# Four rows per partition in the q and k loads, a second matmul 24 steps behind the first, and loads four quads ahead

## The chip, the cores and the metric

The kernel runs on one core of a Trainium2 chip. The metric is the device time of one execution in microseconds (us). The kernel before takes 485.05 us (median of three runs, 484.16 to 485.57). The engines are called as the profile calls them: PE is TensorE's matmuls, PEld its weight loads, DVE is VectorE, ACT is ScalarE, POOL is GpSimd, and SP is the engine that issues the stores.

## The reference

Windowed attention with 32 global tokens per batch feeds a two-layer block with a quick GELU. The global tokens attend to everything; the 512 local tokens of each head attend to the global ones and to a window of 32 on both sides.

```python
# B=8, H=8 heads, Sl=512 local tokens, Sg=32 global tokens, D=64; d_model=512, d_ff=2048
k_all = concat([k_g, k_l]);  v_all = concat([v_g, v_l])
out_g = softmax(scale * q_g @ k_all.T) @ v_all
s_ll  = where(abs(i - j) <= 32, scale * q_l @ k_l.T, -1e9)
out_l = softmax(concat([scale * q_l @ k_g.T, s_ll])) @ concat([v_g, v_l])
x = concat([out_g, out_l])            # 8 * 544 = 4352 tokens of 512
h = x @ w_in
out = (h * sigmoid(1.702 * h)) @ w_out
```

## The kernel before

The kernel works on "quads", four heads of one batch, 16 quads in all. The batches' attention is interleaved with the two big matmuls of the block before it: a "block" is 512 tokens, a "step" is 128 of the 2048 hidden features. There are 8.5 blocks of 16 steps.

The loads put 16 consecutive rows of k (or q) of one head into one partition, 2 KB per partition, one DMA issue for each tensor:

```python
    qf = q_l.rearrange("b (u j) (r t) d -> (b u) (j r) (t d)", j=4, t=16)
    kf = k_l.rearrange("b (u j) (r t) d -> (b u) (j r) (t d)", j=4, t=16)
    ...
    def load(Q):
        rk = ld.tile([128, 16 * D], BF16, name="rk")
        nc.gpsimd.dma_start(out=rk, in_=kf[Q])
        rq = ld.tile([128, 16 * D], BF16, name="rq")
        nc.gpsimd.dma_start(out=rq, in_=qf[Q])
```

The scores need k and q with the features on the partitions. DVE's stream transpose turns every block of 32x32 elements. A block holds the rows `r` of one `t`, so its results belong 16 elements apart in the sequence. They are written with a stride of 16 bf16 elements, 32 bytes:

```python
    def quad(Q):
        ...
        kT = att.tile([128, 2, Sl], BF16, name="kT")
        qT = att.tile([128, 2, Sl], BF16, name="qT")
        for dst, src in ((kT, rk), (qT, rq)):
            nc.vector.transpose(
                dst.rearrange("p h (r t) -> p h t r", t=16),
                src.rearrange("p (t h d) -> p h t d", t=16, h=2),
            )
        ... # s = k.q on PE, exp on ACT, mask on DVE, sums and values on PE, xT = ov * rs on DVE
```

The two big matmuls need DVE as well. Each step fills a PSUM buffer `hp` (there are two), ACT takes its tanh, and DVE makes `gT` from both. Only when `gT` is written is `hp` free for the next step but one:

```python
    def h_step(i, fc):
        ...
        hp = psH.tile([128, TB], F32, name="hp")           # two buffers
        for kc in range(NKC):                               # four matmuls of 128x512
            nc.tensor.matmul(hp[:, :n], lhsT=w_in_sb[:, kc, ...], rhs=xT[:, kc, t0 : t0 + n], ...)
        nc.scalar.activation(th[:, :n], hp[:, :n], AF.Tanh, scale=0.851)
        nc.vector.scalar_tensor_tensor(gTs[i][:, fc, :n], in0=th[:, :n], scalar=1.0, in1=hp[:, :n], ...)

    for i in range(NBK + 1):
        ...
        for st in range(FC):                                # 16 steps
            if i < NBK: h_step(i, st)
            if i > 0:   o_step(i - 1, st)                   # second matmul, 16 steps behind
            ...                                             # and a piece of the next batch's attention
```

The softmax here doesn't subtract the row's maximum and nothing guards it: scores larger than these inputs give would overflow.

## Time and profile before

| | before |
|---|---|
| time | 485.05 us |
| span of the profiled execution | 482.6 us |
| mean granted clock of PE | 0.88 |
| PE busy | 363.7 us (75%) |
| DVE busy | 340.5 us (71%) |
| POOL busy | 112.5 us (23%) |

No engine is full over the whole span, so the average names no limit. One has to look at the stages. The first lines are of the page of the kernel before: busy time of the engines (share of the span, x instructions), then the span in 40 slices (busy tenths, and the clock granted to PE in tenths), then the chain of waits that ended last.

```profile
PE 363.7 (75%) x2913; PEld 184.5 (38%) x2960; DVE 340.5 (71%) x412; ACT 165.6 (34%) x307; POOL 112.5 (23%) x154
PE   0585476764677977599577977599559999999995
PEclk9995595786897997799887998799797999999999
PE 55%; DVE 33%; issue 7%; ACT 3%; DMA 1%; DVEq 0%; ACTq 0%; POOLq 0%
```

PE is full only in the last fifth, where no attention is left. Until then its clock drops again and again. The windows view of the same kernel shows this as three stages: block 0 with what precedes it, blocks 1 to 5, and the rest. Its columns are the window, its length, the busy time of PE, PEld, DVE, ACT and POOL with their instructions, the granted clock, the share of the DMA engines and GB/s.

```profile
0.00:124.00 124.00, 68.37 (x594) 36.27 (x602) 103.44 (x110) 31.38 (x57) 81.23 (x108) 0.78 0.88 96
124.00:383.10 259.10, 202.21 (x1685) 100.87 (x1714) 195.51 (x230) 92.99 (x171) 31.31 (x46) 0.88 0.28 42
383.10:482.60 99.50, 93.13 (x635) 47.40 (x644) 41.53 (x75) 41.28 (x79) 0.00 (x0) 1.00 0.11 41
```

The lines of the groups view give busy time and mean ns of one, then the engine's idle time just before them and what ended it.

```profile
L304 PE MATMUL hp<-xT,w_in_sb 128*128 128x512 bf16 (+1 forms) x535 | 154.2, 401 | 77.9 <-DVE gT L308 65.9
L196 DVE STREAM_TRANSPOSE kT<-rk 128x1024 bf16<-128x1024 bf16 x16 | 72.3, 4519 | 2.8 <-DMA rk<-in_k_l_dram 1.4
L196 DVE STREAM_TRANSPOSE qT<-rq 128x1024 bf16<-128x1024 bf16 x16 | 73.3, 4580 | 0.0
L74 POOL DMA_DIRECT2D rk<-in_k_l_dram x16 | 9.3, 581 | 70.4 <-DVE kT L196 66.6
L76 POOL DMA_DIRECT2D rq<-in_q_l_dram x16 | 8.9, 554 | 34.1 <-DVE qT L196 29.3
```

The 32 transposes take 4.5 us each, 146 us of DVE. PE waits 65.9 us for `gT`. How the one makes the other is seen in the timeline (start, us, engine and line, operation, and in brackets the idle time before it). First a pair of transposes on DVE, then what such a pair does to PE elsewhere:

```profile
282.20 0.68 DVE L308 SCALAR_TENSOR_TENSOR gT<-th,hp 128x512 bf16<-128x512 f32 x1
282.80 4.53 DVE L196 STREAM_TRANSPOSE kT<-rk 128x1024 bf16<-128x1024 bf16 x1
286.98 4.63 DVE L196 STREAM_TRANSPOSE qT<-rq 128x1024 bf16<-128x1024 bf16 x1
291.26 1.06 DVE L242 TENSOR_TENSOR e_2728<-e_2728,mask 128x1408 bf16<-128x1408 bf16 x1
292.25 0.66 DVE L308 SCALAR_TENSOR_TENSOR gT<-th,hp 128x512 bf16<-128x512 f32 x1
```

```profile
231.41 1.03 PE L320 MATMUL op<-w_out_sb,gT 128*128 128x512 bf16 x4
238.40 1.86 PE L304 MATMUL hp<-xT,w_in_sb 128*128 128x512 bf16 x4 [5.97 <-DVE gT L308]
```

For 9.4 us (from 282.88 to 292.25) DVE writes no `gT`, PE stands for 5.97 us, and the four matmuls after it take 1.86 us instead of 1.03. There are two such pairs in a block. So a block with transposes takes 52 to 55 us. The start of a block is read from its first tanh in the timeline, less 0.9 us.

### The profile page before, as it was taken

How to read it: one execution, taken by the hardware profiler on the slowest of the kernel's cores; microseconds unless marked ns; L12 is line 12 of the kernel's file. 1: busy time of each engine (PE TensorE's matmuls, PEld its weight loads, DVE VectorE, ACT ScalarE, POOL GpSimd, SP SyncE). 2: the span in 40 equal slices, each digit the busy share in tenths (PEclk: the TensorE clock that was granted, in tenths of full speed). 3: DMA queues.
4: the chain of work that ended last, by engine and by line, in shares of the span. 5: the costliest groups of instructions: out<-in, count | busy, mean ns of one | idle time of the engine just before them, and what ended most of it. 6: DMA issues, size and time to landing. Idle time of an engine off the chain costs nothing.

```text
span 482.6 us, 7101 instructions
## 1 busy us (share of the span) xinstructions
PE 363.7 (75%) x2913; PEld 184.5 (38%) x2960; DVE 340.5 (71%) x412; ACT 165.6 (34%) x307; POOL 112.5 (23%) x154
## 2 busy tenths in 40 slices
PE   0585476764677977599577977599559999999995
PEld 0253133332233533255233543255224555444552
DVE  7957869998986677866986778876796566633330
ACT  1330153231341372225331372126231374334341
POOL 9655992196101300022001210022000000000000
PEclk9995595786897997799887998799797999999999
DMA  9999894090513432344302433044000100011111
GB/s 116 113 141 198 111 118 57 2 109 6 61 34 58 47 46 57 66 45 45 67 7 58 50 43 64 22 46 46 22 24 0 45 23 23 24 42 46 44 45 65
DMA packets 55905, 26.96 MB, mean 56 GB/s; under 512 B 44352, under 2 KB 46400, under 8 KB 55872
## 3 DMA queue, kind: packets, MB, share of 16 engines
q0 software_dynamic: 50976, 17.58, 34.5%
q1 hardware_dynamic: 4896, 8.92, 4.9%
q8 instruction: 23, 0.38, 0.3%
q14 instruction: 10, 0.08, 0.1%
HBM read 35.13 MB, written 8.91 MB: 91 GB/s over the span
## 4 chain that ended last, share of the span: by engine, by line
PE 55%; DVE 33%; issue 7%; ACT 3%; DMA 1%; DVEq 0%; ACTq 0%; POOLq 0%
PE op L320 21%; PE hp L304 21%; DVE qT L196 15%; DVE kT L196 9%; PE ov L263 4%; DVE gT L308 3%; PE s L214 3%; PE ov L256 2%; PE s L236 2%; DVE e_1041 L242 2%; PE og L280 2%; DVE xT L276 1%; DMA rk<-in_k_l_dram 1%; DVE xg L288 1%; ACT ob L324 1%
## 5 line engine op out<-in xcount | busy, mean ns | idle before, releaser
L304 PE MATMUL hp<-xT,w_in_sb 128*128 128x512 bf16 (+1 forms) x535 | 154.2, 401 | 77.9 <-DVE gT L308 65.9
L307 ACT ACTIVATE th<-hp 128x512 f32<-128x512 f32 (+1 forms) x144 | 83.2, 579 | 240.3 <-PE hp L304 240.2
L320 PE MATMUL op<-w_out_sb,gT 128*128 128x512 bf16 x538 | 148.0, 398 | 2.0 <-ACT ob L324 1.4
L308 DVE SCALAR_TENSOR_TENSOR gT<-th,hp 128x512 bf16<-128x512 f32 (+1 forms) x144 | 94.0, 655 | 76.5 <-ACT th L307 75.9
L304 PEld LDWEIGHTS <-w_in_sb 128*128 128x128 bf16 x576 | 54.8, 102 | 137.8 <-issue 95.0
L320 PEld LDWEIGHTS <-gT 128*128 128x128 bf16 x544 | 55.5, 102 | 69.4 <-issue 14.7
L196 DVE STREAM_TRANSPOSE kT<-rk 128x1024 bf16<-128x1024 bf16 x16 | 72.3, 4519 | 2.8 <-DMA rk<-in_k_l_dram 1.4
L196 DVE STREAM_TRANSPOSE qT<-rq 128x1024 bf16<-128x1024 bf16 x16 | 73.3, 4580 | 0.0
L214 PE MATMUL s<-qT,kT 32*128 32x160 bf16 (+1 forms) x512 | 28.2, 263 | 29.3 <-DVE qT L196 29.3
L214 PEld LDWEIGHTS <-kT 32*128 32x128 bf16 x512 | 15.0, 100 | 48.1 <-issue 23.3
L276 DVE TENSOR_TENSOR xT<-ov,rs 128x512 bf16<-128x512 f32 x32 | 22.1, 690 | 11.8 <-PE ov L263 11.7
L324 ACT ACTIVATE ob<-op 128x512 f32<-128x512 f32 x34 | 20.6, 605 | 15.2 <-PE op L320 15.2
L74 POOL DMA_DIRECT2D rk<-in_k_l_dram x16 | 9.3, 581 | 70.4 <-DVE kT L196 66.6
L84 POOL DMA_DIRECT2D v_89<-in_v_l_dram x16 | 11.9, 754 | 49.2 <-PE og L282 48.4
L288 DVE TENSOR_SCALAR xg<-og,rg 32x64 bf16<-32x64 f32 x64 | 17.9, 280 | 1.2
L270 DVE STREAM_TRANSPOSE sT<-ov 128x512 f32<-128x512 f32 x16 | 11.6, 725 | 7.6 <-PE ov L263 7.6
L76 POOL DMA_DIRECT2D rq<-in_q_l_dram x16 | 8.9, 554 | 34.1 <-DVE qT L196 29.3
L84 POOL DMA_DIRECT2D v_91<-in_v_l_dram x16 | 12.0, 768 | 20.6 <-PE og L282 20.6
L256 PEld LDWEIGHTS <-vgU 128*128 128x128 bf16 x128 | 12.4, 111 | 11.0 <-issue 5.9
L84 POOL DMA_DIRECT2D v_87<-in_v_l_dram x16 | 12.1, 796 | 16.9 <-PE og L282 16.9
L236 PE MATMUL s<-qgBD,kT 128*128 128x128 bf16 x128 | 15.7, 242 | 0.0
L84 POOL DMA_DIRECT2D v_85<-in_v_l_dram x16 | 12.0, 778 | 15.7 <-PE og L282 15.7
(335 smaller groups left out, 346.7 us busy)
## 6 DMA issues: line engine op xcount, KB each, us to landing
out_dram<-ob SPq DMA_DIRECT2D x34, 256.0 KB, 2.0
rk<-in_k_l_dram POOLq DMA_DIRECT2D x16, 256.0 KB, 4.5
rq<-in_q_l_dram POOLq DMA_DIRECT2D x16, 256.0 KB, 3.8
w_in_sb<-in_moe_w_in_dram POOLq DMA_DIRECT2D x8, 256.0 KB, 13.2
w_out_sb<-in_moe_w_out_dram POOLq DMA_DIRECT2D x4, 512.0 KB, 10.8
v_85<-in_v_l_dram POOLq DMA_DIRECT2D x16, 64.0 KB, 3.1
v_87<-in_v_l_dram POOLq DMA_DIRECT2D x16, 64.0 KB, 3.3
v_89<-in_v_l_dram POOLq DMA_DIRECT2D x16, 64.0 KB, 2.8
```

The source lines that it names most:

```text
L84: nc.gpsimd.dma_start(out=v[:, :, j * D : (j + 1) * D], in_=vf[Q, j])
L196: nc.vector.transpose(dst.rearrange("p h (r t) -> p h t r", t=16), src.rearrange("p (t h d) -> p h t d", t=16, h=2),)
L214: nc.tensor.matmul(ps[j][:, col : col + wd], lhsT=kT[p, h, 128 * c : 128 * c + 128], rhs=qT[p, h, q0 : q0 + wd], start=(h == 0), stop=(h = ...
L236: nc.tensor.matmul(o, lhsT=l(h), rhs=r(h), start=(h == 0), stop=(h == 1), skip_group_check=True)
L256: nc.tensor.matmul(ov[:, q0 : q0 + wd], lhsT=lg, rhs=e, start=(i == 0), stop=False, skip_group_check=True)
L276: nc.vector.tensor_mul(xT[:, 2 * u + h, t0 + Sg : t0 + S], ov, rs)
L288: nc.vector.tensor_scalar_mul(xg[p, :], og[p, j * D : (j + 1) * D], rg[p, j : j + 1])
L304: nc.tensor.matmul(hp[:, :n], lhsT=w_in_sb[:, kc, fc * 128 : (fc + 1) * 128], rhs=xT[:, kc, t0 : t0 + n], start=(kc == 0), stop=(kc == NKC ...
L307: nc.scalar.activation(th[:, :n], hp[:, :n], AF.Tanh, scale=0.851)
L308: nc.vector.scalar_tensor_tensor(gTs[i][:, fc, :n], in0=th[:, :n], scalar=1.0, in1=hp[:, :n], op0=ALU.add, op1=ALU.mult)
L320: nc.tensor.matmul(ops[i], lhsT=gTs[i][:, fc, tci * 128 : tci * 128 + 128], rhs=w_out_sb[:, fc, :], start=(fc == 0), stop=(fc == FC - 1))
L324: nc.scalar.activation(ob, ops[i], AF.Copy, scale=0.5)
```

## The change

Its intent is to make the transposes cheap. Four rows instead of 16 lie in a partition, so the results of one 32x32 block belong four elements apart: the write stride falls from 32 to 8 bytes. Since a tensor's rows of a quad are now in four pieces per partition, each load becomes four issues of 64 KB. Around it, loads are issued four quads ahead instead of two, the second matmul runs 24 steps behind the first instead of 16, `xg` is scaled on ACT instead of DVE, `gT` has three buffers instead of two, and the global tokens' tables are kept for three batches instead of all eight, with their last load after `w_out`.

```diff
-    kf = k_l.rearrange("b (u j) (r t) d -> (b u) (j r) (t d)", j=4, t=16)
+    kf = k_l.rearrange("b (u j) (n r t) d -> (b u) j r n (t d)", j=4, n=4, t=4)
...  # q_l likewise; pool "ld" 3 -> 4 buffers
     def load(Q):
-        rk = ld.tile([128, 16 * D], BF16, name="rk")
-        nc.gpsimd.dma_start(out=rk, in_=kf[Q])
...
+        for name, src in (("rk", kf), ("rq", qf)):
+            r = ld.tile([128, 4, 4 * D], BF16, name=name)
+            for n in range(4):
+                nc.gpsimd.dma_start(out=r[:, n, :], in_=src[Q, :, :, n, :])
...
         for dst, src in ((kT, rk), (qT, rq)):
             nc.vector.transpose(
-                dst.rearrange("p h (r t) -> p h t r", t=16),
-                src.rearrange("p (t h d) -> p h t d", t=16, h=2),
+                dst.rearrange("p h (n r t) -> p h n t r", n=4, t=4),
+                src.rearrange("p n (t h d) -> p h n t d", t=4, h=2),
             )
...
-    load_g(2, NQ)
     load(2)
+    load_g(2, 4)
     load_v(2)
+    load(3)
+    load_v(3)
     for g4 in range(4):
         nc.gpsimd.dma_start(out=w_out_sb[...], ...)
-    transpose_g(2, NQ)
+    load_g(4, NQ)
+    transpose_g(2, 4)
...
-        if Q + 2 < NQ and Q + 2 not in loaded:
-            load(Q + 2)
-            load_v(Q + 2)
+        if Q + 4 < NQ:
+            load(Q + 4)                       # and load_v(Q + 4) at the quad's end
...
-            nc.vector.tensor_scalar_mul(xg[p, :], og[p, ...], rg[p, j : j + 1])
+            nc.scalar.activation(xg[p, :], og[p, ...], AF.Copy, scale=rg[p, j : j + 1])
...
+    LAG = 24
+    for k in range(NBK * FC + LAG):
+        i, st = divmod(k, FC)
...
+            h_step(i, st)
+        if 0 <= k - LAG < NBK * FC:
+            o_step(*divmod(k - LAG, FC))
```

More of the change, by code (lines that the diff above doesn't have):

```diff
@@ L54 @@
     wts = ctx.enter_context(tc.tile_pool(name="wts", bufs=1))
-    ld = ctx.enter_context(tc.tile_pool(name="ld", bufs=3))
+    ld = ctx.enter_context(tc.tile_pool(name="ld", bufs=4))
     att = ctx.enter_context(tc.tile_pool(name="att", bufs=2))
@@ L61 @@
     psO = ctx.enter_context(tc.tile_pool(name="psO", bufs=1, space=bass.MemoryType.PSUM))
-    qf = q_l.rearrange("b (u j) (r t) d -> (b u) (j r) (t d)", j=4, t=16)
-    kf = k_l.rearrange("b (u j) (r t) d -> (b u) (j r) (t d)", j=4, t=16)
+    qf = q_l.rearrange("b (u j) (n r t) d -> (b u) j r n (t d)", j=4, n=4, t=4)
+    kf = k_l.rearrange("b (u j) (n r t) d -> (b u) j r n (t d)", j=4, n=4, t=4)
     vf = v_l.rearrange("b (u j) (c p) d -> (b u) j p c d", j=4, p=128)
@@ L72, in load @@
     def load(Q):
-        rk = ld.tile([128, 16 * D], BF16, name="rk")
-        nc.gpsimd.dma_start(out=rk, in_=kf[Q])
-        rq = ld.tile([128, 16 * D], BF16, name="rq")
-        nc.gpsimd.dma_start(out=rq, in_=qf[Q])
-        loaded[Q] = [rk, rq, None]
+        got = []
+        for name, src in (("rk", kf), ("rq", qf)):
+            r = ld.tile([128, 4, 4 * D], BF16, name=name)
+            for n in range(4):
+                nc.gpsimd.dma_start(out=r[:, n, :], in_=src[Q, :, :, n, :])
+            got.append(r)
+        loaded[Q] = got + [None]
     vtiles = []
@@ L132 @@
     kgT = consts.tile([128, NQ, 2, 32], BF16)
-    qgBD = consts.tile([128, NQ, 2, 128], BF16)
-    kgBD = consts.tile([128, NQ, 2, 128], BF16)
-    vgU = consts.tile([128, NQ, 2, 128], BF16)
-    vgBD = consts.tile([128, NQ, 4 * D + 4], BF16)
-    for j in range(4):
-        nc.vector.tensor_copy(vgBD[:, :, 4 * D + j : 4 * D + j + 1],
-                              bdm[:, j : j + 1, 0:1].to_broadcast([128, NQ, 1]))
+    GB = []
+    for i in range(3):
+        kgBD = consts.tile([128, 2, 2, 128], BF16, name="kgBD%d" % i)
+        qgBD = consts.tile([128, 2, 2, 128], BF16, name="qgBD%d" % i)
+        vgU = consts.tile([128, 2, 2, 128], BF16, name="vgU%d" % i)
+        vgBD = consts.tile([128, 2, 4 * D + 4], BF16, name="vgBD%d" % i)
+        for j in range(4):
+            nc.vector.tensor_copy(vgBD[:, :, 4 * D + j : 4 * D + j + 1],
+                                  bdm[:, j : j + 1, 0:1].to_broadcast([128, 2, 1]))
+        GB.append((kgBD, qgBD, vgU, vgBD))
     def transpose_g(lo, hi):
@@ L156, in bd @@
             )
-        m = lambda t: t[:, qs].rearrange("p a h c -> p (a h) c")
-        bd(m(kgBD), m(kgT), 4, 32)
-        bd(m(qgBD), m(qgT), 4, 32)
+        kgBD, qgBD, vgU, vgBD = GB[b % 3]
+        m = lambda t: t.rearrange("p a h c -> p (a h) c")
+        bd(m(kgBD), m(kgT[:, qs]), 4, 32)
+        bd(m(qgBD), m(qgT[:, qs]), 4, 32)
         bd(m(vgU), rvg[:, qs, :].rearrange("p a (h d) -> p (a h) d", h=2), 4, 32)
-        bd(vgBD[:, qs, : 4 * D], rvg[:, qs, :], 2, D)
+        bd(vgBD[:, :, : 4 * D], rvg[:, qs, :], 2, D)
     transpose_g(0, 2)
@@ L181 @@
         )
-    transpose_g(2, NQ)
-    expand_g(1, nc.gpsimd)
+    load_g(4, NQ)
+    transpose_g(2, 4)
+    expand_g(1, nc.vector)
     xT = consts.tile([128, NKC, n_tokens], BF16)
@@ L191, in quad @@
         rk, rq, v = loaded[Q]
+        kgBD, qgBD, vgU, vgBD = GB[b % 3]
         t0 = b * S
@@ L196, in quad @@
             nc.vector.transpose(
-                dst.rearrange("p h (r t) -> p h t r", t=16),
-                src.rearrange("p (t h d) -> p h t d", t=16, h=2),
-            )
-        if u == 0 and b + 2 < B:
-            expand_g(b + 2, nc.gpsimd)
-        if Q + 2 < NQ and Q + 2 not in loaded:
-            load(Q + 2)
-            load_v(Q + 2)
+                dst.rearrange("p h (n r t) -> p h n t r", n=4, t=4),
+                src.rearrange("p n (t h d) -> p h n t d", t=4, h=2),
+            )
+        if Q + 4 < NQ:
+            load(Q + 4)
         E = []
@@ L224, in quad @@
                 full.append((ps[i][:, LW : LW + 128], lambda h, c=c: kT[:, h, 128 * c : 128 * c + 128],
-                             lambda h: qgBD[:, Q, h, :]))
-            kgl = lambda h: kgBD[:, Q, h, :]
+                             lambda h: qgBD[:, u, h, :]))
+            kgl = lambda h: kgBD[:, u, h, :]
             if rnd == 0:
-                full.append((ps[2][:, LW : LW + 128], kgl, lambda h: qgBD[:, Q, h, :]))
+                full.append((ps[2][:, LW : LW + 128], kgl, lambda h: qgBD[:, u, h, :]))
                 full.append((ps[2][:, 480:512], kgl, lambda h: qT[:, h, 480:512]))
@@ L253, in quad @@
             h = unit - 1
-            lg = onesBD if unit == 0 else vgU[:, Q, h, :]
+            lg = onesBD if unit == 0 else vgU[:, u, h, :]
             for i, (e, q0, wd) in enumerate(pieces):
@@ L281, in quad @@
                              start=(c == 0), stop=False)
-        nc.tensor.matmul(og, lhsT=E[0][:, 2, LW : LW + 128], rhs=vgBD[:, Q, :], start=False, stop=True)
+        nc.tensor.matmul(og, lhsT=E[0][:, 2, LW : LW + 128], rhs=vgBD[:, u, :], start=False, stop=True)
         rg = att.tile([128, 4], F32, name="rg")
@@ L287, in quad @@
             p = slice(32 * j, 32 * j + 32)
-            nc.vector.tensor_scalar_mul(xg[p, :], og[p, j * D : (j + 1) * D], rg[p, j : j + 1])
+            nc.scalar.activation(xg[p, :], og[p, j * D : (j + 1) * D], AF.Copy, scale=rg[p, j : j + 1])
         nc.vector.transpose(xT[:, 2 * u : 2 * u + 2, t0 : t0 + Sg],
                             xg.rearrange("p (h d) -> p h d", h=2))
+        if Q + 4 < NQ:
+            load_v(Q + 4)
         yield
@@ L300, in h_step @@
         if fc == 0:
-            gTs[i] = moe.tile([128, FC, TB], BF16, name="gT")
+            gTs[i] = moe.tile([128, FC, TB], BF16, name="gT", bufs=3)
         hp = psH.tile([128, TB], F32, name="hp")
@@ L328, in batch @@
     def batch(b):
+        if b == 1:
+            transpose_g(4, NQ)
+        if 1 <= b < B - 1:
+            expand_g(b + 1, nc.gpsimd)
         a, c = quad(2 * b), quad(2 * b + 1)
@@ L331, in batch @@
             yield next(g, None)
+    LAG = 24
+    NP = 12
     for _ in batch(0):
         pass
-    for i in range(NBK + 1):
-        g = batch(i + 1) if i + 1 < B else iter(())
-        done = 0
-        for st in range(FC):
-            if i < NBK:
-                h_step(i, st)
-            if i > 0:
-                o_step(i - 1, st)
-            while done * FC < (st + 1) * 12 and done < 12:
-                next(g, None)
-                done += 1
+    g = iter(())
+    for k in range(NBK * FC + LAG):
+        i, st = divmod(k, FC)
+        if st == 0:
+            g = batch(i + 1) if i + 1 < B else iter(())
+            done = 0
+        if i < NBK:
+            h_step(i, st)
+        if 0 <= k - LAG < NBK * FC:
+            o_step(*divmod(k - LAG, FC))
+        while done * FC < (st + 1) * NP and done < NP:
+            next(g, None)
+            done += 1
 _INS = ['q_l', 'k_l', 'v_l', 'q_g', 'k_g', 'v_g', 'moe_w_in', 'moe_w_out']
```

## The prediction

> **What bounds the kernel now.** Neither engine is full (page: PE busy 75%, DVE 71%), but two stages differ. From about 115 us to 384 us every 512-token block takes 52 to 55 us. A block without transposes (384 to 420 us in the timeline) takes only 36.5 us, with TensorE busy throughout: 32 groups of four 128x512 matmuls at 0.863 us (27.6 us) plus about 9.3 us of attention matmuls. So TensorE's floor is about 37 us per block. The other 17 us are DVE's: the groups view has 32 stream transposes at 4.52 and 4.58 us; they run in pairs, 8.8 us in which no gT is written, so hp's two PSUM buffers stay full. The waits view has PE hp waiting for DVE gT 65.9 us in 14 waits, up to 6.4 us. After each stall the clock is low: four matmuls take 1.86 us instead of 1.03. That is 2 x (6 + about 2.6) = 17 us per block. The page "TensorE: Matmul & The Clock Gate", Part 1, says that an idle window of about 3.4 us lowers the clock; the trace agrees.
>
> **What the change does.**
> - Transposes. They now write with a 32-byte stride, 4.4 ns per element; the dense 128x896 kgT transpose took 1.10 us, 1.2 ns per element. The Trainium skill ("SBUF — State Buffer", note on cachelines) says that lines have 16 bytes and need two hits each for full rate: an 8-byte stride gives two. No run here shows it yet. Estimate: 1.25 us each, 105 us less DVE work in all. A pair then takes 2.5 us, and gT is again written before TensorE needs its buffer.
> - xg moves to ScalarE: 64 x 0.28 us off DVE, about 64 x 0.22 us onto ScalarE (34% busy): free.
> - Loads: q and k become 128 issues instead of 32, about 0.55 us each: 53 us more on GpSimd (23% busy), harmless in steady state. At the start w_in is issued some 7 us later. DMA engine time hardly grows (a 2 KB packet took 217 ns, four of 512 B about 4 x 60).
> - Lag 24 instead of 16: TensorE's work is the same; eight steps of the second matmul move from the start to the end, where psO's single buffer costs about 0.7 us per four steps. It lets w_out land later.
>
> **Sum.** Batch 0: first block's matmuls in earnest at about 44 us instead of 57, as four of its transposes fall from 4.5 to 1.25 us and the next pair no longer delays it. Blocks 0 and 1, 57 to 170 us now, I put at 44 to 108: limited by loads (w_out and the fourth batch's q and k landing near 70 us) and DVE. Blocks 2 to 6: 5 x 37.5. Block 7 27.6, block 8 21, the last 16 steps 17, store 2: 363. Frictions (GpSimd's multiplies blocking DVE's mask multiplies, as in the 8.2 us one; small PSUM waits): about 9. Predicted 372 us, 8 in 10 between 353 and 399. Faster by over 2% 0.97, within 2% 0.02, slower 0.01.
>
> **What would show it.** Groups view: transposes 1.1 to 1.5 us. Waits: PE hp for DVE gT under 15 us. Timeline: 37 to 39 us per block, granted clock mean near 0.95. The chain of waits: over 80% PE, DVE under 12%. TensorE still mostly busy at about 310 to 340 us.
>
> **What would make it wrong.** Transposes at about 2.3 us (two lines still cost): some 20 us more. DVE queued behind the late global-token transposes (their load is now last): 10 to 20 us more. Four issues per tensor starving the first two blocks of data. Or start stages that overlap better than I think: 355.

## The result, and the profile after

The changed kernel takes 413.26 us (median of four runs, 412.90 to 413.52), and its result is right. The ratio to the kernel before is 0.8515 (95% interval 0.8495 to 0.8536). Ratios are computed as the mean time of one kernel's fast runs over that of the other's of the same rounds, so they are not quite the ratio of the medians quoted. The direction was right, and the time lies outside the predicted range of 353 to 399 us.

The lines of the page of the changed kernel that answer to those of before, with the row of POOL added:

```profile
PE 343.2 (83%) x2911; PEld 177.2 (43%) x2960; DVE 252.0 (61%) x362; ACT 184.0 (45%) x371; POOL 179.6 (44%) x249
PE   0665597677979987998899889988999999999985
POOL 8973993799999999445734002200000000000000
PEclk9999759699889998999999999999999999999999
PE 47%; POOL 19%; DVE 12%; DMA 8%; issue 7%; ACT 6%; DVEq 0%; ACTq 0%; POOLq 0%
```

The clock is nearly recovered (mean 0.963 after 0.88). DVE's part of the chain has fallen from 33% to 12%. POOL, which was not in it at all, has 19% and is nearly full for the first 40% of the span: it is busy for 114.88 of the 134.70 us before block 2. The windows view of the changed kernel, cut at the starts of blocks 2 and 7 (the DMA share adds up the times of all packets, so it can pass 1):

```profile
0.00:134.70 134.70, 91.77 (x844) 48.37 (x857) 93.35 (x143) 51.78 (x106) 114.88 (x166) 0.90 1.06 98
134.70:340.70 206.00, 188.28 (x1756) 97.83 (x1785) 140.19 (x187) 108.92 (x221) 64.77 (x84) 0.99 0.39 51
340.70:411.50 70.80, 63.13 (x313) 31.04 (x318) 18.46 (x34) 23.28 (x46) 0.00 (x0) 1.00 0.13 49
```

The prediction had put the start of block 2 at 108 us and these five blocks at 187.5 us. The groups of the changed kernel:

```profile
L313 PE MATMUL hp<-xT,w_in_sb 128*128 128x512 bf16 (+1 forms) x533 | 144.5, 380 | 31.1 <-DVE gT L317 27.3
L206 DVE STREAM_TRANSPOSE kT<-rk 128x1024 bf16<-128x1024 bf16 x16 | 39.5, 2471 | 10.4 <-DMA rk<-in_k_l_dram 8.7
L206 DVE STREAM_TRANSPOSE qT<-rq 128x1024 bf16<-128x1024 bf16 x16 | 39.4, 2465 | 0.8 <-DMA rq<-in_q_l_dram 0.7
L77 POOL DMA_DIRECT2D rk<-in_k_l_dram x64 | 43.6, 690 | 17.6 <-DVE kT L206 6.6
L77 POOL DMA_DIRECT2D rq<-in_q_l_dram x64 | 42.4, 669 | 9.0 <-DMA w_in_sb<-in_moe_w_in_dram 4.3
```

A transpose takes 2.47 us, twice the 1.25 us of the prediction. The loads of q and k take 86 us of POOL, after 18.2 us before (9.3 + 8.9). The timeline of a pair of transposes, DVE first and then PE:

```profile
225.78 2.47 DVE L206 STREAM_TRANSPOSE kT<-rk 128x1024 bf16<-128x1024 bf16 x1
228.04 2.49 DVE L206 STREAM_TRANSPOSE qT<-rq 128x1024 bf16<-128x1024 bf16 x1
230.34 0.91 DVE L249 TENSOR_TENSOR e_2807<-e_2807,mask 128x1408 bf16<-128x1408 bf16 x1
231.18 0.67 DVE L317 SCALAR_TENSOR_TENSOR gT<-th,hp 128x512 bf16<-128x512 f32 x1
```

```profile
228.95 1.03 PE L329 MATMUL op<-w_out_sb,gT 128*128 128x512 bf16 x4
231.90 1.02 PE L313 MATMUL hp<-xT,w_in_sb 128*128 128x512 bf16 x4 [1.92 <-DVE gT L317]
```

The pair still makes PE wait, now 1.92 us instead of 5.97. The four matmuls after it take no longer than the four before it (1.03 us), so what is lost is the wait alone. The Trainium skill ("TensorE: Matmul & The Clock Gate", Part 1) says that the clock falls after an idle window of about 3.4 us. These two stalls agree: 1.86 us for four matmuls after a stall of 5.97 us, 1.02 us after one of 1.92 us. The traces show no sharp limit for the length of a stall, though: in the kernel before, one of 2.98 us (at 105.23 us) was also followed by 1.86 us, in the changed kernel one of 2.84 us by 1.02 us.

The waits view of the changed kernel (total us, times, longest) has three lines that matter:

```profile
PE hp L313 <- DVE gT L317: 27.3, 13, 5.3
ACT xg L295 <- DVE rg L291: 20.4, 14, 7.0
DVE xT L296 <- ACT xg L295: 20.2, 15, 1.6
```

Before, the first of them was 65.9 us. The last two are new: `xg` now goes from DVE to ACT and back, and DVE stands 1.3 us each time (20.2 / 15).

The stages, in us. "Before 0" is the time until block 0 starts. The last column is all that follows block 7.

| kernel | before 0 | block 0 | block 1 | block 2 starts | block 2 | blocks 3, 4, 5 | block 6 | block 7 | rest |
|---|---|---|---|---|---|---|---|---|---|
| before | 52.2 | 71.8 | 43.9 | 167.9 | 54.4 | 54.6, 52.2, 53.9 | 37.6 | 27.3 | 34.6 |
| after | 52.9 | 44.3 | 37.5 | 134.7 | 43.5 | 41.6 each | 37.9 | 27.4 | 43.3 |

The gain of 71 us in the span splits into 33.2 us before block 2 and 46.8 us in blocks 2 to 6, less 8.7 us in the rest. The miss splits as well: block 2 starts 26.7 us later than predicted, blocks 2 to 6 take 18.5 us more, the rest 3.3 us more than the 40 predicted. Against these stand the 9 us that the prediction had added for frictions. (The median time is 1.8 us longer than the span, which makes up the sum of 41.3 us.)

Why the start is slow is told by the chain of waits up to the start of block 2. First before (up to the start of its block 1, 124 us), then after:

```profile
by line: DVE qT L196 21.3%; DVE kT L196 20.5%; DVE e_1041 L242 6.6%; issue 6.2%; PE hp L304 6.0%; PE s L214 5.8%; DVE gT L308 4.7%; DVE xT L276 3.8%; PE s L236 3.7%; PE ov L263 3.3%; DMA rk<-in_k_l_dram 2.9%; DVE xg L288 2.6%; PE ov L256 2.
```

```profile
by line: POOL rq L77 12.7%; POOL rk L77 12.1%; DMA w_in_sb<-in_moe_w_in_dram 10.5%; DMA rkg<-in_k_g_dram 9.8%; POOL v_85 L86 6.4%; POOL v_87 L86 4.4%; issue 4.2%; PE hp L313 4.0%; DVE qT L206 3.6%; DMA rq<-in_q_l_dram 2.9%; DVE gT L317 2.3%
```

In place of the transposes, the act of issuing loads and the landing of `w_in` and of the global tokens' `rkg` make up most of the chain at the start. In the timeline of POOL in the changed kernel an issue also has to wait for landings:

```profile
31.52 0.67 POOL L77 DMA_DIRECT2D rk<-in_k_l_dram  x1 [3.42 <-DMA w_in_sb<-in_moe_w_in_dram]
33.55 1.99 POOL L77 DMA_DIRECT2D rk<-in_k_l_dram  x3 [1.36 <-DMA w_in_sb<-in_moe_w_in_dram]
39.84 2.65 POOL L77 DMA_DIRECT2D rq<-in_q_l_dram  x4 [4.30 <-DMA w_in_sb<-in_moe_w_in_dram]
```

The `w_in` that released the last of these was issued at 25.44 us and took 14.1 us to land. Counted in the timeline, it is the eighth issue before it; the same holds for the other two. So the trace shows at most eight loads of this queue under way at once. The framework sets that number: in the program that the run's kernel.py builds to, its loads from POOL use eight semaphores in turn, and each issue is told to wait for the landing of the eighth before it. Eight loads of 64 KB hold a quarter of the data of eight of 256 KB; what that costs by itself is not measured.

### The profile page after: what moved, and what is told of

Read it like the earlier page. It is cut to its first block, busy times and chain, and to the rows that moved or that the text cites. A ratio compares the mean times of both kernels' runs of the same rounds, so it can differ in the third digit from the quotient of the medians.

```text
span 411.5 us, 7258 instructions
## 1 busy us (share of the span) xinstructions
PE 343.2 (83%) x2911; PEld 177.2 (43%) x2960; DVE 252.0 (61%) x362; ACT 184.0 (45%) x371; POOL 179.6 (44%) x249
## 3 DMA queue, kind: packets, MB, share of 16 engines
q0 software_dynamic: 114000, 17.79, 49.8%
## 4 chain that ended last, share of the span: by engine, by line
PE 47%; POOL 19%; DVE 12%; DMA 8%; issue 7%; ACT 6%; DVEq 0%; ACTq 0%; POOLq 0%
PE op L329 22%; PE hp L313 17%; POOL rq L77 5%; POOL rk L77 4%; DVE qT L206 4%; DMA w_in_sb<-in_moe_w_in_dram 3%; DMA rkg<-in_k_g_dram 3%; PE ov L270 3%; DVE kT L206 3%; DVE gT L317 2%; POOL v_85 L86 2%; PE ov L263 2%; ACT ob L333 1%; POOL v_87 L86 1%; ACT xg L295 1%
## 5 line engine op out<-in xcount | busy, mean ns | idle before, releaser
L313 PE MATMUL hp<-xT,w_in_sb 128*128 128x512 bf16 (+1 forms) x533 | 144.5, 380 | 31.1 <-DVE gT L317 27.3
L329 PE MATMUL op<-w_out_sb,gT 128*128 128x512 bf16 x538 | 139.1, 382 | 5.1 <-ACT ob L333 4.6
L329 PEld LDWEIGHTS <-gT 128*128 128x128 bf16 x544 | 53.3, 98 | 67.0 <-issue 8.6
L77 POOL DMA_DIRECT2D rk<-in_k_l_dram x64 | 43.6, 690 | 17.6 <-DVE kT L206 6.6
L77 POOL DMA_DIRECT2D rq<-in_q_l_dram x64 | 42.4, 669 | 9.0 <-DMA w_in_sb<-in_moe_w_in_dram 4.3
L206 DVE STREAM_TRANSPOSE kT<-rk 128x1024 bf16<-128x1024 bf16 x16 | 39.5, 2471 | 10.4 <-DMA rk<-in_k_l_dram 8.7
L221 PE MATMUL s<-qT,kT 32*128 32x160 bf16 (+1 forms) x512 | 26.1, 257 | 19.4 <-DVE qT L206 18.5
L206 DVE STREAM_TRANSPOSE qT<-rq 128x1024 bf16<-128x1024 bf16 x16 | 39.4, 2465 | 0.8 <-DMA rq<-in_q_l_dram 0.7
L221 PEld LDWEIGHTS <-kT 32*128 32x128 bf16 x512 | 14.1, 98 | 36.6 <-issue 19.1
L295 ACT ACTIVATE xg<-og,rg 32x64 bf16<-32x64 f32 x64 | 19.5, 305 | 21.2 <-DVE rg L291 20.4
L296 DVE STREAM_TRANSPOSE xT<-xg 128x64 bf16<-128x64 bf16 x16 | 3.9, 246 | 20.2 <-ACT xg L295 20.2
L281 DVE STREAM_TRANSPOSE rs<-rT 128x512 f32<-128x512 f32 x16 | 11.4, 711 | 0.5
```

Source lines behind the costliest of these rows:

```text
L77: nc.gpsimd.dma_start(out=r[:, n, :], in_=src[Q, :, :, n, :])
L206: nc.vector.transpose(dst.rearrange("p h (n r t) -> p h n t r", n=4, t=4), src.rearrange("p n (t h d) -> p h n t d", t=4, h=2),)
L221: nc.tensor.matmul(ps[j][:, col : col + wd], lhsT=kT[p, h, 128 * c : 128 * c + 128], rhs=qT[p, h, q0 : q0 + wd], start=(h == 0), stop=(h = ...
L295: nc.scalar.activation(xg[p, :], og[p, j * D : (j + 1) * D], AF.Copy, scale=rg[p, j : j + 1])
L313: nc.tensor.matmul(hp[:, :n], lhsT=w_in_sb[:, kc, fc * 128 : (fc + 1) * 128], rhs=xT[:, kc, t0 : t0 + n], start=(kc == 0), stop=(kc == NKC ...
L329: nc.tensor.matmul(ops[i], lhsT=gTs[i][:, fc, tci * 128 : tci * 128 + 128], rhs=w_out_sb[:, fc, :], start=(fc == 0), stop=(fc == FC - 1))
```

## The experiments

My theory had two parts. The transposes cost 2.47 us because bf16 writes at 8 bytes are not at full rate, and that makes the stalls in blocks 2 to 6. And POOL's 128 issues, which I had called harmless, delay the first blocks. The rivals: the longer access pattern of the transpose costs the time, not its stride; or the other parts of the change do harm, namely the lag of 24, `xg` on ACT, or the late load of the global tokens.

Twelve kernels ran. Four of them (`e1_dense`, `e2_oneload`, `e3_both`, `e12_four_big`) permute rows of q and k and are wrong. The comparison with the reference passed them all the same, because with these inputs the scores are so small that the softmax is almost uniform. In a functional simulation with q and k ten times larger, the kernels before and after have a relative error of 0.0047, `e1_dense` and `e3_both` of 1.1. `e5_strides` is wrong too. The same simulation gave 0.0047 for the pair transposes of `e9_pair_before` and `e11_pair_best`.

The medians, with the ratio to the kernel before in the same rounds:

| run | what it is | us | ratio (95%) |
|---|---|---|---|
| before | | 485.31 | 1 |
| after | | 413.26 | 0.8515 (0.8495 to 0.8536) |
| e1_dense | after, transposes write densely | 394.17 | 0.8094 (0.8050 to 0.8138) |
| e2_oneload | after, one issue per tensor | 396.47 | 0.8135 (0.8068 to 0.8201) |
| e3_both | both of these | 375.51 | 0.7718 (0.7674 to 0.7762) |
| e4_xg_dve | after, xg back on DVE | 410.87 | 0.8428 (0.8366 to 0.8490) |
| e6_lag16 | after, lag 16 | 411.81 | 0.8495 (0.8438 to 0.8551) |
| e7_g_early | after, global tokens loaded before w_out | 408.32 | 0.8413 (0.8359 to 0.8466) |
| e8_before_tr | before, with only the new loads and transposes | 407.79 | 0.8391 (0.8350 to 0.8433) |
| e9_pair_before | before, with transposes of pairs | 367.40 | 0.7537 (0.7481 to 0.7594) |
| e10_pair_after | after, with transposes of pairs, one issue | 374.60 | 0.7684 (0.7645 to 0.7724) |
| e11_pair_best | e10 with the harmful parts taken back | 364.26 | 0.7473 (0.7436 to 0.7511) |
| e12_four_big | after, eight issues of 2 KB packets | 406.72 | 0.8361 (0.8318 to 0.8404) |

Two of these had runs marked slow: one of six of `e2_oneload` (402.68) and two of four of `e9_pair_before` (373.46 and 375.72). They are left out of medians and ratios. So `e9_pair_before` rests on two fast runs. What made the slow ones slow is not known: their clock was nearly the same (0.981 and 0.977, against 0.984 and 0.986).

The kernel before was measured again with each set of runs, and its median lay between 485.31 and 488.38 us. So a difference between medians of different sets, such as the changed kernel's against an experiment's, is good to 2 or 3 us only. The experiments `e2_oneload`, `e3_both`, `e4_xg_dve`, `e6_lag16`, `e7_g_early` and `e12_four_big` also got another order of instructions from the framework's scheduler than the changed kernel has; `e1_dense` kept it.

### Dense writes: what the stride alone costs

```diff
-                dst.rearrange("p h (n r t) -> p h n t r", n=4, t=4),
+                dst.rearrange("p h (n t r) -> p h n t r", n=4, t=4),
```

> The changed kernel with one edit: the 32 transposes write densely (wrong result on purpose, k and q are permuted; loads and instruction order unchanged). Theory A (the 8-byte stride still halves the write rate, and the 4.95 us pair is what stops TensorE twice per block): transposes 1.25 us instead of 2.47, blocks 3 to 5 fall from 41.6 to about 37.7 us, waits of the first matmul for gT from 27 us to under 8 us, total about 396 us. Rival B (DVE waiting for ScalarE's xg and the masks is what stops TensorE in a block): transposes fall but the blocks stay at 41 us, total above 407 us.

The access pattern keeps its number of dimensions, and all other instructions keep their order on every engine. The group of the transposes (by form) and the wait of `hp` in `e1_dense`:

```profile
L206 DVE STREAM_TRANSPOSE kT<-rk 128x1024 bf16<-128x1024 bf16 x16 | 19.9, 1242 | 15.7 <-DMA rk<-in_k_l_dram 14.7 <-PE s L243 0.9
PE hp L313 <- DVE gT L317: 10.6, 5, 4.9
```

The time is 394.17 us, 19.1 less. The transpose takes 1.24 us, which is the number that the prediction had for the 8-byte stride. Blocks 3 to 6 take 37.9 us each, so 3.7 us (41.6 - 37.9) of a block were the stride's. Block 2 starts at 132.2 us, only 2.5 us earlier, though each transpose there is half as long. So the first blocks were not waiting for transposes. That is the first part of the theory shown, and the second supported. One expectation was missed: PE's waits for `gT` fell to 10.6 us and not below 8, nearly all of it in two waits of 4.95 and 4.36 us before block 2.

### One issue per tensor, and both edits

```diff
-    kf = k_l.rearrange("b (u j) (n r t) d -> (b u) j r n (t d)", j=4, n=4, t=4)
+    kf = k_l.rearrange("b (u j) (r t) d -> (b u) (j r) (t d)", j=4, t=16)      # q_l likewise
-            for n in range(4):
-                nc.gpsimd.dma_start(out=r[:, n, :], in_=src[Q, :, :, n, :])
+            nc.gpsimd.dma_start(out=r.rearrange("p n w -> p (n w)"), in_=src[Q])
```

`e3_both` has this edit and the one before it.

> The changed kernel with q and k loaded by one issue per tensor again (16 rows per partition) while the transposes still write as if four rows lay in a partition (wrong result on purpose). Theory C (GpSimd's issue of four loads per tensor, in one queue with the weights and the block-diagonal multiplies, limits the first 135 us): block 2 begins at about 115 us instead of 135, total about 392 us; transposes stay at 2.47 us. Rival D (the start is limited by the transposes and the DMA engines, not by issues): block 2 begins later than 128 us, total above 405 us.

> Both edits: dense transposes and one issue per tensor (wrong result on purpose). If A and C together are what the prediction lacked, 366 to 380 us. If something else is missing (the xg round trip, the late global-token load, the tail), above 385 us.

`e2_oneload` takes 396.47 us, 16.8 less. Its transposes still take 2.46 us and its blocks 2 to 5 still 41.6 us, but block 2 starts at 122.8 us, 11.9 earlier. That lies between what theory C (about 115) and rival D (later than 128) had said; the total is near C's 392 and clear of D's 405. So C holds, with a smaller effect than expected. The profiled run was one of the two slower ones of the five fast (399.42; the others 395.69 to 396.47), so its stages hold only 13.8 us of the 16.8. The framework's scheduler put its instructions in another order on POOL, DVE, PE and ACT, so a part of the 16.8 us may be the order's. `e2_oneload` and `e3_both` have the same order, and between them the dense writes are worth 21 us.

`e3_both` takes 375.51 us, 3.5 us from the prediction. Block 2 starts at 113.5 us and blocks 2 to 6 take 37.9 us each. The two terms together are 37.8 us of the 41.3 us that were missed. They are not merely added: at the start, where the two edits alone gain 2.5 and 11.9 us, both together gain 21.2 us. Only when data arrives in time do the first blocks wait for transposes.

### Large packets in eight issues: the number of issues or their packets

```diff
-                nc.gpsimd.dma_start(out=r[:, n, :], in_=src[Q, :, :, n, :])
+                nc.gpsimd.dma_start(out=r[32 * n : 32 * n + 32].rearrange("p n w -> p (n w)"), in_=src[Q, 32 * n : 32 * n + 32])
```

with `qf` and `kf` as in `e2_oneload`. There are still eight issues per quad, each of 64 KB, but with 32 packets of 2 KB instead of 128 of 512 bytes.

> The run with one issue per tensor changed two things against the changed kernel: 2 issues instead of 8 per quad, and DMA packets of 2048 instead of 512 bytes. This one keeps 8 issues but has the large packets: the 16-row layout, loaded by 32 partitions at a time; transposes write with 8 bytes (wrong result on purpose). If the number of issues is what costs: near the changed kernel, 405 to 415 us. If the packet size costs: near the run with one issue per tensor, 395 to 401 us.

The groups of the loads by form, in `e12_four_big` and then in `e2_oneload` (one issue of 256 KB):

```profile
L77 POOL DMA_DIRECT2D rk<-in_k_l_dram x64 | 32.6, 534 | 17.9 <-DVE kT L206 6.5 <-DMA w_in_sb<-in_moe_w_in_dram 5.7 <-DMA w_out_sb<-in_moe_w_out_dram 4.9
```

```profile
L76 POOL DMA_DIRECT2D rk<-in_k_l_dram x16 | 9.6, 600 | 25.6 <-DVE kT L206 17.4 <-DMA w_in_sb<-in_moe_w_in_dram 4.5 <-DVE xT L296 2.9
```

The time is 406.72 us. Of the 16.8 us that one issue gains, 6.5 come with larger packets and some 10 with fewer issues, both good to 2 or 3 us. An issue of 128 rows of 512 bytes takes 0.69 us, one of 32 rows of 2 KB 0.53 us, and one of 128 rows of 2 KB, four times the bytes, 0.60 us. So an issue here is mostly a fixed cost, and the time is nearer to what was expected if the number of issues costs: POOL is busy 157.5 us here, 111.3 us in `e2_oneload`. The larger packets also spare the DMA engines: the queue of all loads took 49.8% of the span in the changed kernel and 41.6% here, that is 205 and 169 us of each engine's time (0.498 x 411.5 and 0.416 x 405.1). More than half of the difference is packets of 4 bytes: the trace of the changed kernel has 49,152 more of them, three for each of its 16,384 packets of 512 bytes, and they take 30.6 us of each engine's time in place of 5.9. What they carry is not shown. The DMA share over the first 122 us is 1.08 in the changed kernel and 0.95 here, so at the start the DMA engines are full as well. Whether the 6.5 us are POOL's shorter issues or the DMA engines' shorter work, this run can't tell. It shares the order caveat of `e2_oneload`.

### The stride by itself

This kernel transposes one loaded tile of 128x1024 elements again and again with nothing else under way, writes zeros to the output, and so is wrong (relative error 1.0). Its core:

```python
    def blocks(x, order):
        return x.rearrange("p (%s) -> p n t r" % order, r=32, t=T)
    for T in (1, 2, 4, 8, 16):                     # bf16, write stride 2*T bytes
        nc.vector.transpose(blocks(w, "n r t"), blocks(a, "n t r"))
    for T in (4, 16):  ...  blocks(b, "t n r"), blocks(a, "n t r")     # dense write, other block order
    for T in (2, 4, 16): ... blocks(g, "n t r"), blocks(a, "n r t")    # read stride 2*T bytes, dense write
    for T in (1, 2, 4, 8): ... blocks(h, "n r t"), blocks(f, "n t r")  # fp32, write stride 4*T bytes
    for T in (1, 2, 4, 8, 16): nc.vector.tensor_copy(blocks(c, "n r t"), blocks(a, "n t r"))
```

> A kernel that does nothing but DVE transposes of 1024 elements per partition (it writes zeros as output, wrong on purpose): bf16 tiles w1 to w16 written with a stride of 1, 2, 4, 8, 16 elements (2 to 32 bytes), b4 and b16 written densely but with the 32-element runs in another order, g2 to g16 read with a stride and written densely, h1 to h8 the same in fp32 (4 to 32 bytes), c1 to c16 plain copies with the write strides. If the cost follows the 16-byte lines of the Trainium skill (two hits per line are enough): 1.25 us up to 8 bytes, more only from 16 bytes on; but the changed kernel already showed 2.47 us at 8 bytes, so I expect a step before 8 bytes: 4 bytes either 1.25 us (the limit lies between 4 and 8 bytes) or about 1.6 us (cost grows with each doubling). If the access pattern's number of dimensions costs and not the stride, b4 and b16 are as slow as w4 and w16; I expect them at 1.25 us.

It ran once (139.13 us, state unknown for a single run). The page merges the strides of a group, so these are the durations of single instructions in the timeline, in us for 1024 elements per partition. The framework let neighbouring strides alternate; the order of the instructions in the built program says which is which. A transpose with a stride of 8 bytes, one of 16 bytes, and a dense one with the blocks in another order (`b4`):

```profile
16.56 2.39 DVE L63 STREAM_TRANSPOSE w<-a 128x1024 bf16<-128x1024 bf16 x1
18.76 4.72 DVE L63 STREAM_TRANSPOSE w<-a 128x1024 bf16<-128x1024 bf16 x1
47.75 1.41 DVE L67 STREAM_TRANSPOSE b<-a 128x1024 bf16<-128x1024 bf16 x1
```

All of them, by stride:

| stride | 2 B | 4 B | 8 B | 16 B | 32 B |
|---|---|---|---|---|---|
| bf16 transpose, strided write | 1.19 to 1.25 | 1.26 | 2.39 to 2.63 | 4.72 | 4.40 to 4.65 |
| bf16 transpose, strided read, dense write | | 1.20 | 1.21 | | 1.97 |
| fp32 transpose, strided write | | 1.21 | 1.21 | 1.95 | 1.99 |
| bf16 copy, strided write | 0.42 | 0.74 | 1.3 to 1.5 | 2.48 | 2.30 to 2.54 |

A dense write with the blocks in another order takes 1.20 to 1.41 us, so the number of dimensions is not the cost. The stride is. In bf16 a write at 8 bytes is half the rate and at 16 or 32 bytes a quarter. The same 8 bytes cost nothing in fp32, nor in bf16 on the reading side. This is where the step of the prediction was wrong: it took a rule of two accesses per 16-byte line from the Trainium skill ("SBUF — State Buffer", the note on cachelines) and applied it to bf16 writes. Two bf16 writes per 16 bytes were not enough here. Four were.

### The other parts of the change

`e4_xg_dve` puts `xg` back on DVE, `e6_lag16` sets the lag to 16, `e7_g_early` loads the last global tokens before `w_out`, each in the changed kernel:

```diff
-            nc.scalar.activation(xg[p, :], og[p, j * D : (j + 1) * D], AF.Copy, scale=rg[p, j : j + 1])
+            nc.vector.tensor_scalar_mul(xg[p, :], og[p, j * D : (j + 1) * D], rg[p, j : j + 1])
```

> The changed kernel with xg computed on DVE again. DVE gets 64 x 0.28 us of work back but no longer waits 16 x 1.3 us for ScalarE. If moving xg helped as the prediction said: 2 to 6 us slower. If the move only turned work into a wait of the same length: within 1% (409 to 417 us).

The time is 410.87 us (407.21 to 412.56): no slower with 17.9 us more work on DVE, since the 20.2 us of waiting for ACT are gone. A wait had replaced the work. The medians differ by 0.6%, and the intervals of the two ratios just miss each other.

```diff
-    LAG = 24
+    LAG = 16
```

> The changed kernel with the second matmul 16 steps behind the first instead of 24. If the prediction is right that the lag moves TensorE work only from the start to the end: within 1.5% of 413 us. The tail (from the last first-matmul step on) falls from 43 to about 35 us while blocks 0 and 1 grow by about as much. If the longer lag hides the late landing of w_out: block 1 gets 10 us or more longer and the total is over 416 us. If the lag only costs: below 408 us.

The time is 411.81 us (411.00 to 414.27), the same. The rest after block 7 falls from 43.3 to 34.6 us, but block 2 starts 5.0 us later, at 139.7 us, and takes 44.9 us. So the eight steps moved from one end to the other, and a lag of 24 has no worth of its own here.

```diff
+    load_g(4, NQ)
     for g4 in range(4):
         nc.gpsimd.dma_start(out=w_out_sb[...], ...)
-    load_g(4, NQ)
```

> The changed kernel with the last load of the global tokens issued before w_out instead of after it. If DVE's wait of 5.0 us for that load (with the 5.3 us stall of TensorE behind it and the slow clock after it) lies on the critical path: 4 to 8 us faster, 405 to 409 us. If GpSimd's queue is the limit there: within 2 us of 413.

The time is 408.32 us (407.03 to 410.91), 4.9 or 1.2% less. In the changed kernel DVE stood for this load while it had `gT` to write. Its timeline, DVE and then PE:

```profile
72.11 0.98 DVE L148 STREAM_TRANSPOSE kgT<-rkg 128x768 bf16<-128x768 bf16 x1 [4.99 <-DMA rkg<-in_k_g_dram]
```

```profile
75.37 1.87 PE L313 MATMUL hp<-xT,w_in_sb 128*128 128x512 bf16 x4 [5.33 <-DVE gT L317]
```

This stall is long enough for the clock to fall, and four matmuls take 1.87 us after it. The prediction had listed this as a risk. With the early load this stall is gone, but `e7_g_early` has another 6 us later, where DVE stands for a load of `rk` (DVE, then PE; at this low clock five matmuls take 2.29 us):

```profile
78.35 2.44 DVE L206 STREAM_TRANSPOSE kT<-rk 128x1024 bf16<-128x1024 bf16 x1 [3.37 <-DMA rk<-in_k_l_dram]
81.37 2.29 PE L313 MATMUL hp<-xT,w_in_sb 128*128 128x512 bf16 x5 [4.53 <-DVE gT L317]
```

In all, PE waits 26.8 us for `gT` there, after 27.3. So the run shows a small gain with the earlier load, but not that the stall of 5.33 us was what it cost.

### Only the loads and the transposes, in the kernel before

```diff
# against the kernel before: the new qf, kf, load() and the new transposes as in "The change", nothing else
```

> The kernel before with only the loads of four rows per partition and the 8-byte-stride transposes. If these alone carry the gain in the middle blocks: blocks 2 to 5 fall from 53.8 to 42 to 43 us each, total about 425 to 440 us against 485. If lag, buffers and the fourth load ahead are what keeps TensorE fed: blocks above 46 us, total above 445 us.

The time is 407.79 us (406.89 to 408.01), 5.5 us or 1.3% less than the whole change, and the intervals of the ratios don't overlap. The blocks are as expected, but the total is 17 us below the expected 425 to 440: block 2 starts 26.8 us earlier than in the kernel before, which I had not counted. The rest after block 7 is 34.6 us, blocks 2 to 5 take 41.3 us. Block 2 starts at 141.1 us, 6.4 later than in the changed kernel. So the new loads and transposes alone bring the whole gain. The rest of the change wins 6.4 us at the start and gives back more than that in blocks 2 to 6 (3.1 us) and at the end (8.7 us).

### Transposing pairs: dense enough without small loads

If fp32 writes are cheap and bf16 writes are not, then two neighbouring features of one row can be moved as one 32-bit word. 512 words are transposed instead of 1024 elements, and each partition then holds features 2w and 2w+1 in place of w and w+32. The two accumulating matmuls of the scores take even and odd features in place of lower and upper halves. The sum is the same, and it needs the loads of the kernel before, 16 rows per partition in one issue.

```diff
-        kT = att.tile([128, 2, Sl], BF16, name="kT")            # qT likewise
+        kT = att.tile([128, Sl, 2], BF16, name="kT")
         for dst, src in ((kT, rk), (qT, rq)):
             nc.vector.transpose(
-                dst.rearrange("p h (r t) -> p h t r", t=16),
-                src.rearrange("p (t h d) -> p h t d", t=16, h=2),
+                dst.rearrange("p s h -> p (s h)").bitcast(F32).rearrange("p (r t) -> p t r", t=16),
+                src.bitcast(F32).rearrange("p (t w) -> p t w", t=16),
             )
...  # matmuls read kT[p, s, h] for kT[p, h, s]; the global tokens' transposes likewise,
...  # followed by a copy that parts the pairs
```

`e9_pair_before` is this in the kernel before, `e10_pair_after` this and one issue per tensor in the changed kernel. `e11_pair_best` is `e10_pair_after` with the global load early, `xg` on DVE, a lag of 16, and the global tokens' block tables made on DVE instead of POOL.

> The kernel before with one edit of a different kind (right result): loads as they were (16 rows per partition, one issue per tensor), but a transpose moves pairs of bf16 as 512 fp32 words, written with a 64-byte stride; the two accumulating matmuls then take the even and the odd features instead of the two halves. The stride run has 1024 fp32 words at a 32-byte stride in 1.97 us, so if the cost goes by words, 0.95 to 1.1 us each. If DVE's transposes and GpSimd's issues are together what the middle blocks and the start pay for, this alone gets what the whole change was predicted to get: blocks 2 to 5 at 37.6 to 38 us, total 368 to 378 us. If TensorE reads of every second element cost something, its matmuls of s grow beyond 265 ns and the blocks beyond 38.5 us.

> The changed kernel with the same transposes of pairs and one issue per tensor (right result): lag 24, xg on ScalarE, loads four ahead stay. Its two limits are then gone as in the run with both edits: 368 to 377 us. Compared with the run before it, it shows what the rest of the change is worth once neither limit is there: I expect less than 5 us either way.

> The same with what the other runs showed to cost nothing or to help: global tokens' last load before w_out, xg on DVE, lag 16, and the block-diagonal multiplies on DVE instead of GpSimd. Blocks 2 to 6 at TensorE's floor of 37.5 us, tail 35 us, total 358 to 368 us. If the multiplies on DVE (1.6 us per block) stop TensorE: blocks above 38.5 us and total above 370 us.

The transposes in `e9_pair_before`, then the page's line of busy engines and of the chain in `e11_pair_best`:

```profile
L198 DVE STREAM_TRANSPOSE kT<-rk 128x512 f32<-128x512 f32 x16 | 16.7, 1047 | 8.1 <-DMA rk<-in_k_l_dram 6.8 <-PE s L238 1.3
```

```profile
PE 337.8 (93%) x2960; PEld 175.6 (48%) x2960; DVE 233.9 (64%) x456; ACT 165.3 (46%) x307; POOL 83.8 (23%) x129
PE 70%; DVE 9%; ACT 7%; DMA 6%; POOL 6%; issue 2%; POOLq 0%; ACTq 0%
```

A transpose takes 1.05 us, less than a dense one of bf16, although it writes with a stride of 64 bytes. The score matmuls, which now read every second element, are no slower: 245 and 261 ns for the two widths, just as in `e3_both`, where they read neighbouring elements at much the same granted clock (0.984 and 0.970). A cost of reading every second element is not seen. The fast runs of `e9_pair_before` take 367.0 and 367.8 us, with 37.7 us in blocks 2 to 6 and PE waiting 0.5 us for `gT` in all. All three results are right.

`e10_pair_after` at 374.60 us is slower than the fast runs of `e9_pair_before`, by 7.2 us and not by less than 5 as expected. Again the other parts of the change don't help; its rest after block 7 is 43.3 us, that of `e9_pair_before` 34.6. `e11_pair_best` has the lowest time, 364.26 us (363.98 to 364.59), and beats both kernels: 0.7473 of the time before, 0.88 of the time after (364.26 / 413.26). Its lead over `e9_pair_before` is under 1%, and the intervals of the two ratios overlap. Its start still waits for `w_in`: the longest piece of its chain is 15.99 us of `w_in` landing, and block 0 starts at 46.9 us.

## Why the prediction was right or wrong

**What bounds the kernel before: right.** The pairs of transposes hold back `gT`, PE stands, and the clock falls. Making the transposes cheaper alone took 78 us off with the new loads (`e8_before_tr`) and 118 us with the old ones (`e9_pair_before`). TensorE's floor of 37 us a block was right too: 37.7 to 38.3 us a block with transposes in every kernel in which they no longer stall PE.

**The clock recovers: right.** I had expected a mean near 0.95 and it is 0.963, after 0.88.

**"Estimate: 1.25 us each": wrong, the first failing step.** They measured 2.47 us, and the micro kernel gave 2.39 to 2.63 us at this stride. The estimate of 105 us less DVE work was 67 us (145.6 - 78.9). Hence "gT is again written before TensorE needs its buffer" fell as well: PE waits 27.3 us for `gT`, not under 15, and blocks 2 to 6 take 206.0 us, not 187.5. `e1_dense`, with transposes of the predicted length, has 189.8 us there. The failure was named in advance ("transposes at about 2.3 us: some 20 us more"), and 19.1 us is what it was. The range should have given it more room: the rule had never been seen in a trace of this case.

**"53 us more on GpSimd, harmless in steady state": wrong at the start, the second failing step.** The issues cost 0.69 and 0.67 us each, not 0.55, so 68 us more (86.0 - 18.2). After block 2 they do no harm, but few are left by then: blocks 3 to 5 take 41.6 us each with 16 issues of q and k in that stretch or with 4 (`e2_oneload`). Of the 128 issues 85 come before block 2 starts and 27 in block 2. But the loads of the first four quads, `w_in` and `w_out` all pass through this one engine in the first 59 us, one after the other. I put the first block's matmuls at 44 us (from 57, counted to where they run without gaps) and block 2 at 108. By the measure of the table above block 0 starts at 52.9 us, no earlier than before (52.2), and block 2 at 134.7. "Four issues per tensor starving the first two blocks of data" was among my reasons for being wrong, without a size. `e2_oneload` gives it 16.8 us (with another order of instructions), of which `e12_four_big` puts 6.5 on small packets, be it in issuing or in moving them.

**"DMA engine time hardly grows": too low.** The queue of all loads has 49.8% of a shorter span after 34.5% of a longer one, that is 205 us after 166 us of each engine's time, nearly a quarter more; its packets grew from 50,976 to 114,000. The prediction had four packets of 512 bytes at 4 x 60 ns in place of one of 217 ns; they took 69 ns each, and it had not reckoned with the 4-byte packets that came with them, nearly four fifths of the new packets. From block 2 on this binds nothing (a DMA share of 0.39). At the start the engines were nearly full before (0.88 over the first 124 us) and are full now (1.08 over the first 122 us).

**"xg moves to ScalarE: free": wrong in reason, small in effect.** It took 17.9 us of work off DVE and gave it 20.2 us of waiting. `e4_xg_dve` is not slower.

**Lag 24 neutral: right. Late global load a risk: too high.** `e6_lag16` is the same. The stall came, 5.33 us of PE, but `e7_g_early` gains 4.9 us at most without it, where I had feared 10 to 20. The rest after block 7 took 43.3 us, 3.3 more than predicted.

**The chain "over 80% PE, DVE under 12%": wrong for PE.** It is 47% PE with POOL and DMA taking 27%. That was the sign that the start, not the steady state, held the larger part of the miss.

The sum holds nearly: with transposes of the predicted length and the extra issues taken away altogether, `e3_both` takes 375.5 us against 372 predicted. (The prediction had kept the issues and called them harmless.) What stays open is the share of issuing and of moving small packets in the 6.5 us of `e12_four_big`, how much of the gain of `e2_oneload`, `e3_both` and `e12_four_big` belongs to the other order of instructions that came with the edit, and whether `e11_pair_best` is faster than `e9_pair_before` at all. No run issued the loads from an engine other than POOL, which would have parted POOL's time from that of the DMA engines.

## What to carry to other kernels

Measure the cost of a strided write in its own type and on its own engine before you build a data layout on it; a wider word, here two bf16 as one fp32, can buy the cheap write without touching the loads. Count the issues that a layout needs on the engine that issues them, and look at the first blocks apart from the steady state: an engine that is 44% busy on average, as POOL is in the changed kernel, can still be the one that much waits for at the start. Work that is moved to an idle engine from between two instructions of a busy one can leave a wait as long as the trip there and back: here 20.2 us of waiting for 17.9 us of work.

## What the Trainium skill lacked or had wrong

- "SBUF — State Buffer", the note on cachelines and the line of the specifications: two hits per 16-byte line do not give VectorE full rate for bf16 writes. A bf16 transpose with an 8-byte write stride takes 2.39 to 2.63 us alone and 2.47 us in the kernel, a dense one 1.19 to 1.25 us, a 4-byte stride 1.26 us. A bf16 copy behaves alike (0.42, 0.74 and 1.3 to 1.5 us at 2, 4 and 8 bytes). For fp32 writes (1.21 us at 8 bytes, 1.95 at 16) and bf16 reads (1.21 us at 8 bytes) the rule agrees with the runs.
- "VectorE: DVE Perf Modes", section "The three transpose paths": it gives one figure for VectorE's transpose, 311 ns for 128x128 bf16, and none by write stride. The runs show a factor of almost four between 2 and 16 bytes (1.19 to 4.72 us for 128x1024), and that pairs of bf16 moved as fp32 words take 1.05 us at a stride of 64 bytes.
- "DMA: Bandwidth & Descriptors", section "Anatomy of one DMA — SWDGE (gpsimd) path": it calls descriptor generation "small, variable". Here an issue of a load held GpSimd for 0.53 us with 32 rows of 2 KB and 0.69 us with 128 rows of 512 bytes, the same 64 KB, and 128 of the latter for 86 us. The same page's rule to coalesce many small transfers (section "Rules for kernel authors") agrees with the runs: going from 64 KB in 512-byte packets to 256 KB in one issue gained 16.8 us (with another order of instructions). No page that I found tells why three packets of 4 bytes, 9 ns each, came with every row of 512 bytes here.
- No page that I found tells of a bound on the loads under way on GpSimd's queue. In this trace an issue waits for the landing of the one eight before it, up to 4.30 us at a time. In the built program these waits are the framework's, with eight semaphores in turn; whether the chip has a bound of its own is not shown.
- "TensorE: Matmul & The Clock Gate", Part 1, agreed: stalls of 5.97 and 5.33 us were followed by four matmuls of 1.86 and 1.87 us, a stall of 1.92 us by 1.02 us. But one of 2.98 us was followed by 1.86 us too, so the length of a stall alone doesn't tell.
